# A 96-byte constant tile at the top of the right side of SBUF in a kernel of Fourier mixing and a gated feed-forward layer

## The chip, the cores and the metric

The kernel runs on one core of one Trainium2 chip. The metric is the device time of one execution in microseconds (us). Three executions of the kernel before the change took 755.44, 754.17 and 755.10 us; the median is 755.1 us.

## The reference

For an input x of 2048 rows and 512 columns, everything in fp32:

```python
a = x @ dft_hid_re.T                      # (2048, 512)
b = x @ dft_hid_im.T
y = dft_seq_re @ a - dft_seq_im @ b       # DFT matrices of 2048 x 2048
out_b = (silu(x @ w1) * (x @ w3)) @ w2    # w1, w3: 512 x 1376, w2: 1376 x 512
g = sigmoid((x * gate_w).sum(-1))
return g * y + (1 - g) * out_b
```

## The kernel before

**Arithmetic.** Every fp32 operand of a matrix product is split into two parts, a rounded high part (type fp32r) and the rest. `split` (L109) does it: ScalarE copies the source into the high part (L110), VectorE subtracts that from the source for the low part (L111). `mm3` (L113) then issues three matmuls, high by high, high by low and low by high, all at L115. Each has a stationary operand of 128x128 and a moving operand of 128x512, both fp32r in SBUF, and adds into a bank of PSUM. So nearly the whole of TensorE's work is one kind of instruction at one line: a weight load and a matmul of 512 columns, 3,078 times. [...] The products are grouped in a Strassen-like scheme of seven half-size products with sums of operands in front, which VectorE forms.

**Stages.** (1) Gate and up (about 0 to 236 us): the stationary operands are weights (tiles `wa` and `wb`, made from w1 and w3), the moving operand is x transposed, in the large tiles `xo0` for the first 1024 rows and `xo1` for the other 1024. The list ITEMS (L156) sets the order: first nine chunks with `xo0`, then chunks 9 and 10 with both halves in turn, then nine with `xo1`. The first item is done by `plain` (L336) with other small tiles, `b12` and `a21`. Each of the other 21 items is seven products with 42 matmuls in all, into the tiles X, Y and Z. (2) From about 236 us on, 182 steps (`step`, L687) of up to twelve matmuls each, into tiles named P: blocks 0 to 3 multiply with the sequence DFT (the moving operand is `zo`, split from blocks B of the input cc; the stationary operand is `a`, the tiles `a1` and `a2`), blocks 4 and 5 (H) are the product with w2, blocks 6 and 7 (Y) the hidden DFT and the output. A block of the kind F goes through seven products (P1, P5, P6, P3, P7, P2, P4) of four steps each; H has three and Y two steps for each product.

**What sets the order around the matmuls.** TensorE and the DMA queue of SyncE follow the order in which the code issues. In the second part everything does (L567). `advance` (L553), called in each step, loads blocks ahead, forms the sums (`sum_c`, L518) and splits the operand of the step three ahead (`split_c`, L530). There are four `zo` tiles. After the split of a block B22, the queue of GpSimd issues a DMA that adds another block onto it in place (L543); the result is split for the product P7, which comes one product later.

**Where the tiles lie.** SBUF is filled from both ends of each partition: pools opened with side "left" grow from the low end, pools with side "right" from the high end. In the kernel as built, the left side begins at byte 1152, which is 9 x 128. The first tile on the right is the constant `act0` (L118), 128 x 1 fp32, which lies at byte 229,312, which is 64 more than a multiple of 128. Every tile behind it on either side is a multiple of 2048 bytes. So every operand tile on the left starts at a multiple of 128, and every one on the right 64 bytes past one; slices of operands start at multiples of 512 bytes within a tile. On the left lie `xo0`, `b12`, `a21`, two of the four `zo` tiles (`zo_0`, `zo_1`), and seven of the eight tiles `a1` (later those of H and Y in their places). On the right lie `wa`, `wb`, `xo1`, the `zo` tiles `zo_2` and `zo_3`, the eighth `a1`, and all tiles `a2`. A matmul takes its two operands from the same side or from two sides, as these places give it:

- gate and up with `xo0`: moving left, stationary right;
- gate and up with `xo1`: both right;
- second part: all four combinations, in runs of 12 or 24 matmuls.

`act0` itself holds nothing that is used: one Silu (L334) writes it at the start from the zeros of the tile `warm`, and nothing reads it.

Of the kernel before, what the change touches and what calls it, by code (L numbers as in the profile page):

```python
# [7 lines left out]
F32 = mybir.dt.float32  # L8
F32R = mybir.dt.float32r
AF = mybir.ActivationFunctionType  # L10
ALU = mybir.AluOpType

P = 128
# [20 lines left out]
def fnet_swiglu_gate_kernel(  # L34
# [20 lines left out]
    nc = tc.nc  # L55
# [12 lines left out]
    const = ctx.enter_context(tc.tile_pool(name="const", bufs=1, side="right"))  # L68
# [46 lines left out]
            nc.tensor.matmul(ps, u, v, start=first and n == 0, stop=last and n == 2,  # L115
                             skip_group_check=chain)

    act0 = const.tile([P, 1], F32, tag="act0", name="act0")  # L118
    nbsp = dram.tile([D, S], F32, tag="nbsp", name="nbsp")
    gs = dram.tile([NTB, 1, 512], F32, tag="gs", name="gs")  # L120
    gsp, ngsp = (dram.tile([2, P, 1024], F32, tag=k, name=k) for k in ("gsp", "ngsp"))
# [207 lines left out]
    warm = s1p.tile([P, 1024], mybir.dt.bfloat16, tag="s1", name="warm")[:, :512]  # L329
    nc.vector.memset(warm, 0.0)  # L330
    wps = bank(7, "wps")
    for n in range(WARM):
        nc.tensor.matmul(wps, warm[:, :P], warm, start=True, stop=True)
    nc.scalar.activation(act0, warm[:, :1], AF.Silu)  # L334

    def plain(b12, a21):  # L336

# [511 lines left out]
```

## Time and profile before

| what | value |
|---|---|
| median of three executions | 755.1 us (754.17 to 755.44) |
| the profiled execution | 754.2 us; its span 752.4 us |
| granted TensorE clock, mean | 0.993 |
| TensorE matmul busy | 97% of the span, 3,089 matmuls |
| VectorE busy | 76% |
| ScalarE busy | 49% |
| DMA | 186.17 MB, mean 247 GB/s |

The span is the time from the first to the last instruction of the profiled execution; 1.8 us of its time lie outside. A matmul's row has a start and a duration, but matmuls overlap in the pipeline: one of 512 columns is shown with about 390 ns, while the next one starts about 230 ns after it. What a matmul costs the kernel is the distance from start to start, so rows of a timeline that merge six equal matmuls are read by their starts, six distances apart. An idle time at an engine is put down to the instruction whose semaphore came last.

### The profile page before, as it was taken

Reading aid. Unit: us, or ns where it says so; the run is one execution under the profiler, and the core shown is the slowest. Engines: PE = TensorE matmul, PEld = TensorE weight load, DVE = VectorE, ACT = ScalarE, POOL = GpSimd, SP = SyncE. Lnnn points to the kernel's source line nnn. Section 1 sums busy time; section 2 is a strip of 40 time slices with the busy share of each in tenths; the row PEclk is TensorE's granted clock in tenths of the full one; section 3 lists DMA queues with packets and bytes.
Section 4 is the critical chain, followed back from the end, with each engine's and each line's share of the span. In section 5 each row is a group of like instructions: output and inputs, shape, how many; then the busy total and the mean of one; then the engine's idle time right before and its main releaser. Section 6 shows DMA issues by size and latency. Waiting matters only on the chain.

```text
span 752.4 us, 8533 instructions
## 1 busy us (share of the span) xinstructions
PE 726.2 (97%) x3089; PEld 580.0 (77%) x3089; DVE 574.7 (76%) x715; ACT 367.0 (49%) x485; POOL 52.4 (7%) x76
## 2 busy tenths in 40 slices
PE   9999999989897899999999999999999999999996
PEld 5777888878675677888788878887878878887775
DVE  6989895467574997887698769884976695885956
ACT  6665564445433665345453545444435454453423
POOL 0111111101010010001000010001001001000000
PEclk9999999999999999999999999999999999999999
DMA  6575682368869757775957495829999599696862
GB/s 251 172 303 218 249 331 101 108 216 310 326 225 420 263 148 230 267 284 160 267 215 274 134 284 211 309 88 272 360 417 372 153 337 294 219 346 199 310 162 90
DMA packets 49626, 186.17 MB, mean 247 GB/s; under 512 B 5168, under 2 KB 5296, under 8 KB 44976
## 3 DMA queue, kind: packets, MB, share of 16 engines
q1 hardware_dynamic: 39440, 142.10, 52.0%
q0 software_dynamic: 9856, 43.00, 19.3%
q8 instruction: 24, 0.39, 0.2%
q10 hardware_dynamic: 288, 0.52, 0.2%
q14 instruction: 18, 0.15, 0.1%
HBM read 128.45 MB, written 57.16 MB: 247 GB/s over the span
## 4 chain that ended last, share of the span: by engine, by line
PE 31%; issue 24%; DMA 21%; DVE 16%; ACT 6%; SPq 1%; POOL 1%; POOLq 0%; ACTq 0%; DVEq 0%
PE P L115 19%; DMA B<-cc 8%; PE X L115 7%; DVE zo L111 5%; ACT zo L110 4%; DMA B<-zsp 3%; DMA xr<-xn 3%; PE Z L115 3%; DVE B L527 2%; PE Y L115 2%; DMA B<-hsp 1%; DMA dsp<-late 1%; PE C L115 1%; DMA nb<-nbsp 1%; DMA gs<-sc 1%
## 5 line engine op out<-in xcount | busy, mean ns | idle before, releaser
L115 PE MATMUL P<-zo,a 128*128 128x512 f32 x1344 | 314.7, 394 | 8.5 <-DVE zo L111 5.1
L115 PEld LDWEIGHTS P<-zo,a 128*128 128x128 f32 x1344 | 252.2, 188 | 71.1 <-DVE zo L111 10.5
L110 ACT ACTIVATE zo<-B 128x1024 fp32r<-128x1024 f32 (+1 forms) x182 | 187.7, 1043 | 218.1 <-PE P L115 76.7
L111 DVE TENSOR_TENSOR zo<-B,zo 128x1024 fp32r<-128x1024 f32 (+1 forms) x182 | 216.9, 1203 | 98.1 <-ACT zo L110 97.4
L115 PE MATMUL P<-zo,H 128*128 128x512 f32 x468 | 107.9, 392 | 0.2 <-DVE zo L111 0.2
L115 PEld LDWEIGHTS P<-zo,H 128*128 128x128 f32 x468 | 87.7, 188 | 20.2 <-DVE zo L111 0.6
L115 PE MATMUL X<-xo,wb 128*128 128x512 f32 x378 | 95.4, 396 | 4.2 <-DVE u L290 3.2
L527 DVE TENSOR_TENSOR B<-B,B 128x1024 f32<-128x1024 f32 (+1 forms) x78 | 92.8, 1190 | 2.5 <-DMA B<-hsp 2.4
L115 PEld LDWEIGHTS X<-xo,wb 128*128 128x128 f32 x378 | 71.4, 190 | 22.1 <-DVE u L290 4.5
L115 PE MATMUL P<-zo,Y 128*128 128x512 f32 x336 | 80.5, 400 | 3.2 <-ACT zu L726 2.7
L115 PEld LDWEIGHTS P<-zo,Y 128*128 128x128 f32 x336 | 63.8, 191 | 19.8 <-ACT zu L726 3.1
L115 PE MATMUL X<-xo,wa 128*128 128x512 f32 x126 | 33.9, 401 | 3.5 <-ACT h L297 2.7
L115 PE MATMUL Z<-xo,wa 128*128 128x512 f32 x126 | 32.7, 395 | 0.8 <-ACT u L287 0.8
L115 PE MATMUL Y<-xo,wa 128*128 128x512 f32 x126 | 32.6, 393 | 0.0
L115 PE MATMUL Z<-xo,wb 128*128 128x512 f32 x126 | 32.5, 392 | 0.0
L115 PEld LDWEIGHTS X<-xo,wa 128*128 128x128 f32 x126 | 23.7, 190 | 9.8 <-ACT h L297 3.3
L290 DVE TENSOR_TENSOR u<-u,X 128x512 f32<-128x512 f32 x21 | 14.4, 684 | 20.3 <-PE X L115 20.0
L115 PEld LDWEIGHTS Z<-xo,wa 128*128 128x128 f32 x126 | 23.4, 188 | 7.1 <-ACT u L287 1.9
L115 PEld LDWEIGHTS Y<-xo,wa 128*128 128x128 f32 x126 | 23.7, 188 | 5.4
L115 PEld LDWEIGHTS Z<-xo,wb 128*128 128x128 f32 x126 | 23.6, 188 | 5.3
L543 POOL DMA_DIRECT2D B<-cc x16 | 13.7, 858 | 200.5 <-DVE zo L111 186.6
L110 ACT ACTIVATE wa<-ws 128x768 fp32r<-128x768 f32 (+2 forms) x21 | 17.0, 810 | 19.0 <-PE Z L115 11.8
(106 smaller groups left out, 529.5 us busy)
## 6 DMA issues: line engine op xcount, KB each, us to landing
B<-cc SPq DMA_DIRECT2D x64, 512.0 KB, 6.8
hsp<-h POOLq DMA_DIRECT2D x22, 512.0 KB, 5.9
B<-hsp SPq DMA_DIRECT2D x20, 512.0 KB, 9.6
wbsp<-wb POOLq DMA_DIRECT2D x8, 1024.0 KB, 5.7
wb<-wbsp SPq DMA_DIRECT2D x8, 1024.0 KB, 5.2
B<-cc POOLq DMA_DIRECT2D x16, 512.0 KB, 10.4
B<-zsp SPq DMA_DIRECT2D x16, 512.0 KB, 7.7
H<-w2sp SPq DMA_DIRECT2D x6, 1024.0 KB, 10.2
```

The costliest lines, as they stand in the source:

```text
L110: nc.scalar.activation(hi, src, AF.Copy)
L111: nc.vector.tensor_sub(lo, src, hi.bitcast(F32))
L115: nc.tensor.matmul(ps, u, v, start=first and n == 0, stop=last and n == 2, skip_group_check=chain)
L290: nc.vector.tensor_add(u4, u4, x)
L527: nc.vector.tensor_add(t, t, RAW[blk, b, q][:, :n])
L543: nc.gpsimd.dma_start(src, block(blk, "B12", q), accum_op=ALU.add)
```

## The change

The constant tile `act0` takes 24 columns in place of one, 96 bytes in place of 4 in each partition, and the Silu that fills it takes 24 columns of `warm`. The tile of 4 bytes begins at byte 229,312; that of 96 bytes takes 64 bytes more of the allocation and begins at 229,248, which is 1791 x 128. All other tiles of the right side lie 64 bytes lower than before, and so at multiples of 128. The left side is as it was, and the two sides do not meet: the least distance between them is 832 bytes before the change. Nothing else is touched.

```diff
-    act0 = const.tile([P, 1], F32, tag="act0", name="act0")
+
+    act0 = const.tile([P, 24], F32, tag="act0", name="act0")
...
-    nc.scalar.activation(act0, warm[:, :1], AF.Silu)
+    nc.scalar.activation(act0, warm[:, :24], AF.Silu)
```

## The prediction

> **What bounds the kernel now.** I read the engine table first, then the timeline of TensorE in stretches with no stop in them, then the chain that ended last, and last the table by stretches. The page's first line of busy times:
>
> ```profile
> PE 726.2 (97%) x3089; PEld 580.0 (77%) x3089; DVE 574.7 (76%) x715; ACT 367.0 (49%) x485; POOL 52.4 (7%) x76
> ```
>
> TensorE is taken for 97% of the 752.4 us, and it does one thing: a matmul of 512 columns, 3,078 times. Where it isn't stopped, the time of the kernel is the distance from one matmul's start to the next's, times their number. So the question is whether that distance hangs on where the operands lie. The timeline of TensorE in the first product shows it with one moving tile and two stationary ones:
>
> ```profile
> 9.94 2.60 PE L115 MATMUL C<-xo,wa 128*128 128x512 f32 x10 [0.29 <-DVE xo L111]
> 12.38 1.56 PE L115 MATMUL C<-b,wa 128*128 128x512 f32 x6
> 13.78 1.53 PE L115 MATMUL C<-b,a 128*128 128x512 f32 x6
> 15.15 0.63 PE L115 MATMUL C<-xo,wa 128*128 128x512 f32 x2
> ```
>
> Six matmuls of `b12` (left) with `wa` (right) take from 12.38 to 13.78, 1.40 us, 233 ns for each. Six with the same moving tile and `a21` (left as well) take from 13.78 to 15.15, 1.37 us, 228 ns. Longer stretches of the gate and up stage are sharper. First with `xo0` on the left and the weights on the right, then with `xo1` and the weights both on the right:
>
> ```profile
> 60.33 1.56 PE L115 MATMUL Z<-xo,wb 128*128 128x512 f32 x6
> ...
> 74.32 1.56 PE L115 MATMUL Z<-xo,wa 128*128 128x512 f32 x6
> ```
>
> ```profile
> 169.50 1.52 PE L115 MATMUL Z<-xo,wb 128*128 128x512 f32 x6
> ...
> 180.38 1.52 PE L115 MATMUL X<-xo,wa 128*128 128x512 f32 x6
> ```
>
> In the first, 60 matmuls (the rows between are 6, 6, 6, 6, 12, 6, 6 and 6) start within 13.99 us: **233.2 ns**. In the second, 48 (6, 6, 6, 6, 12, 6 and the first 6) start within 10.88 us: **226.7 ns**. Instruction, shapes, types and engine order are equal; what differs is that the operands lie 64 bytes off each other modulo 128 in the first and agree in the second. In `b12` with `a21` both are at 0, in `xo1` with the weights both at 64: that they agree is what the fast pairs have in common, not that they are at 0.
>
> The second part mixes the four combinations. Its longest piece without a stop, from the chain of work that ended last:
>
> ```profile
> 604.06 66.25 PE P L115 x287
> ```
>
> From the first start to the last end 66.25 us; less the 0.16 us by which a last matmul is shown longer than its distance (390 less 230 ns), 66.09 / 287 = **230.3 ns**, between the two values above, as a mixture must be.
>
> **The change part by part.** *The Silu on act0.* It takes 24 columns in place of one. ScalarE's rows at the start:
>
> ```profile
> 2.03 0.20 ACT L334 ACTIVATE act<-warm 128x1 f32<-128x1 bf16 x1
> 3.16 0.42 ACT L110 ACTIVATE wa<-ws 128x256 fp32r<-128x256 f32 x1 [0.93 <-DMA ws<-w]
> ```
>
> One column takes 0.20 us, 256 take 0.42, so 24 take some 0.02 more, in the 0.93 us in which ScalarE waits for its first weights anyway. If that cover went, it would cost 0.02 us. Nothing reads the tile. I count nothing.
>
> *The other engines.* They read and write the moved tiles too. ScalarE's groups by shape, with results on the left (`b`) and on the right (`wb`):
>
> ```profile
> L110 ACT ACTIVATE b<-xs_B 128x1024 fp32r<-128x1024 f32 x1 | 1.1, 1061 | 0.2 <-DMA xs_B<-xt 0.2
> L110 ACT ACTIVATE wb<-wu 128x1024 fp32r<-128x1024 f32 x11 | 11.6, 1057 | 2.3 <-DVE wu L220 2.3
> ```
>
> 1061 ns at 0 and 1057 at 64 modulo 128: no difference to speak of. For VectorE and the DMA queues no row separates the places so cleanly; no instruction is added or moved there, and I count nothing for them, with up to 1 us on either side left to the range.
>
> *The matmuls.* All operands of both sides now agree modulo 128. I take 226.7 ns for every matmul that isn't stopped, the value of pairs that agree, and work out what this takes off TensorE.
> - Gate and up with `xo0`: ten of the 21 items of 42 matmuls, and 36 of the 48 of the first item. 456 x (233.2 - 226.7) = 3.0 us. The items with `xo1` agree already and gain nothing.
> - The second part: 1344 + 468 + 336 = 2,148 matmuls of tiles P. 2,148 x (230.3 - 226.7) = 7.7 us.
>
> That is 10.7 us less work on TensorE, and the upper end. What doesn't reach the end is worked out by stage, from the table by stretches (per row: PE, PEld, DVE, ACT, POOL busy, granted clock, share of DMA, GB/s):
>
> ```profile
> 25.00:60.00 35.00, 32.62 (x138) 25.34 (x137) 31.56 (x45) 22.55 (x31) 3.08 (x5) 1.00 0.65 247
> 202.00:230.00 28.00, 26.22 (x105) 20.76 (x106) 17.34 (x31) 11.21 (x21) 4.17 (x6) 0.94 0.72 254
> 230.00:260.00 30.00, 24.34 (x93) 17.89 (x92) 22.08 (x30) 15.73 (x21) 1.84 (x3) 0.94 0.94 368
> 260.00:300.00 40.00, 39.40 (x169) 31.27 (x168) 32.67 (x43) 23.16 (x33) 3.45 (x4) 1.00 0.63 178
> 500.00:550.00 50.00, 49.24 (x215) 39.82 (x213) 35.10 (x40) 23.84 (x30) 3.42 (x4) 1.00 0.87 283
> 735.00:752.40 17.40, 13.07 (x48) 10.00 (x48) 12.59 (x13) 4.85 (x6) 0.00 (x0) 0.90 0.24 91
> ```
>
> - *25 to 60 us*: VectorE is busy for 31.56 of 35 us, and TensorE stops for 2.4 us. 137 matmuls x 6.5 ns = 0.9 us are to be had; where VectorE is the link, a faster TensorE only stops longer. Of 0.9 I let half go: 0.45 us lost.
> - *230 to 300 us*: the stage changes over; TensorE stands for 5.7 and 0.6 us, and the chain runs through the splits on ScalarE and VectorE and the loads (DMA at 0.94). 262 matmuls x 3.6 ns = 0.9 us, of which I let 0.7 go.
> - *The blocks after it*: TensorE is busy for 49.24 of the 50 us from 500 on, with short stops, and one pattern returns in them. From the chain, in the second block:
>
> ```profile
> 351.73 10.25 DMA B<-cc
> 361.99 0.02 issue
> 362.01 1.07 ACT zo L110
> ...
> 367.78 1.24 DVE zo L111
> 369.01 0.04 issue
> 369.06 3.06 PE P L115 x12
> ```
>
> GpSimd's adding DMA (L543) is issued at 351.73, when the block B22 has been split, takes 10.25 us, and its result must be split before the product P7 can start. Between the two lie one product's four steps of TensorE, 48 matmuls, 11.1 us at 230.3 ns. The DMA and the splits don't get shorter; TensorE's part does, by 48 x 3.6 = 0.17 us, and the stop at P7 grows by as much. One such link in each of the eight blocks: 8 x 0.17 = 1.4 us lost. SyncE's loads are issued further ahead (`advance` loads eight steps ahead); one that comes late costs in the same way and is in the range.
>
> Sum: 10.7 - 0.45 - 0.7 - 1.4 = 8.1 us. From the profiled execution's own 754.2 us that gives 746.1; that execution lies 0.9 us under the median of the three, so the forecast as a median is 755.1 - 8.1 = **747.0 us**, 1.1% faster.
>
> [...]
>
> **The rivals.** *The places don't matter* (what differs between the stretches is something else, such as which tiles VectorE and the DMAs touch meanwhile, or which half of SBUF is read): nothing changes, 755.1 us. For it speaks that pairs from two sides are the slow ones, so that the side itself could be the cause and not the 64 bytes. Against the first reason: the rows of six start 1.40 and 1.36 us apart all through the two stretches, in which the other engines start and stop. Against the second I have only that 64 bytes are a plainer difference than a side. 10 in 100.
>
> *The gain is eaten by loads and splits.* For it: DMA is busy for 0.87 of the stretch 500 to 550 us and 0.94 at the change of stages, and every block's chain goes through DMA waits such as the 10.25 us above. If the whole second part ran at the pace of the DMAs, only the gate and up stage's 3.0 - 0.45 = 2.5 us would stay: 752.6 us. Against it: TensorE stands for less than 2% of that part, so it is still what sets the pace between the stops. With half of the second part's remaining 5.6 us kept, 755.1 - 2.5 - 2.8 = 749.8. 13 in 100, at 749.5 to 753.
>
> *Slower: pairs across the sides meet worse.* All pairs seen to run at 226.7 ns come from one side, where the distance between operands is a multiple of 512 bytes. Across the sides it is now 192 or 320 modulo 512, and after the change it will be 256, which no row shows. If the reads collide by a larger period than 128 bytes, these pairs could fall on a slower step. They are 456 in gate and up and some 1,050 in the second part (counted from the tiles' places). One step of 6.5 ns more than today costs 1,500 x 6.5 = 9.8 us, half a step 4.9; on TensorE's path nothing hides it. Taken in between, nearer to the half: 761 us. It decides from the point where a pair across the sides takes longer than it does today (233.2 ns in gate and up). For it speaks only that the period is unknown; against it, that two places 64 bytes apart already make the whole difference. 7 in 100.
>
> *The clock* changes each of these by a step: in the stretches of 28, 30 and 17.4 us with 0.94, 0.94 and 0.90 the granted clock was down for 28 x 0.06 = 1.7 us of full speed each. If stops shift, one such window may go or come: 1.7 us on either side.
>
> **How the numbers follow.** Forecast 70 in 100, with a range of its own of 747.0 less and plus 2.7 (one clock window, 1 us for loads): 744.3 to 749.7. Gain eaten 13, places don't matter 10, slower 7. The range for 8 in 10 is the forecast's and the eaten gain's, 744.0 to 752.6. A measurement of this kernel can tell about 0.2%, 1.5 us, from no change: faster than that has 70 and 13, 0.83; the same 0.09; slower, with a little of the unchanged cases, 0.08.
>
> **What would show it.** In gate and up with `xo0`, rows of six matmuls should start 1.36 us apart in place of 1.40; those with `xo1` stay at 1.36. A long piece of P in the chain should come to 227 ns for each matmul in place of 230.3. If gate and up quickens and P doesn't, P's pairs are the ones to ask. The starts of P7 should wait longer than now, by about 0.2 us. If the distances fall and the time doesn't, the stops have grown and the gain was eaten; if the distance with `xo0` stays at 233.2, it is the side that counts; above it, the third rival.

## The result and the profile after

The changed kernel takes 749.56 us (median of four executions, 748.86 to 750.54) against 754.85 us before; the ratio is 0.9931 with a 95% interval of 0.9914 to 0.9948, so it is faster by 5.2 us (3.9 to 6.5). The forecast was 747.0 us, 8.1 us faster. Its range holds the result; its size is off by a third, and, as the experiments show, its rule for which places are fast was wrong.

Line numbers from L118 on are one higher than before. TensorE's timeline in gate and up with `xo0`, where six matmuls took 1.40 us:

```profile
59.40 1.52 PE L115 MATMUL Z<-xo,wb 128*128 128x512 f32 x6
60.76 1.52 PE L115 MATMUL X<-xo,wa 128*128 128x512 f32 x6
62.12 1.52 PE L115 MATMUL X<-xo,wb 128*128 128x512 f32 x6
63.48 1.52 PE L115 MATMUL Z<-xo,wa 128*128 128x512 f32 x6
64.84 1.52 PE L115 MATMUL Y<-xo,wa 128*128 128x512 f32 x6
```

24 starts in 5.44 us are 226.7 ns for each, in place of 233.2. The longest pieces of the second part, from the chain that ended last:

```profile
368.50 76.28 PE P L115 x335
...
601.78 70.80 PE P L115 x311
```

(76.28 - 0.16) / 335 is 227.2 ns, the other gives 227.1, where the piece of before gave 230.3. So TensorE's distances did what the prediction said of them, in both stages. The Silu on act0 costs 0.02 us in ScalarE's wait at the start, as expected:

```profile
2.03 0.22 ACT L335 ACTIVATE act<-warm 128x24 f32<-128x24 bf16 x1
3.14 0.42 ACT L110 ACTIVATE wa<-ws 128x256 fp32r<-128x256 f32 x1 [0.89 <-DMA ws<-w]
```

**Where the rest went.** From the starts of the 3,078 matmuls at L115 each trace can be split into three: what distances up to 245 ns hold over 226.7 ns; what longer ones hold in stretches whose granted clock is 0.50 (427 ns for a matmul); and the stops. (The page's other eleven matmuls, at L333, take 1.19 to 5.66 us before the change, most of them 427 ns apart.) In us:

```
trace                      longer distances   half clock   stops   span
before                          10.4              3.8       30.6   752.4
after                            1.3              7.4       32.3   748.8
after, second trace (e1)         1.0              3.3       33.9   745.8
```

The border between the last two columns is good to about 0.8 us, since a matmul can lie partly in a half-speed stretch or behind a stop. The distances give back 9.1 and 9.4 us. The stops take 1.7 and 3.3 of it. The half-speed clock takes 3.6 us more in one trace of the changed kernel and 0.5 less in the other. The table by stretches shows where: before (its row from 230 us on stands in the prediction), after, and the second trace (the numbers behind the busy times are granted clock, share of DMA and GB/s).

```profile
150.00:205.00 55.00, 50.28 (x216) 40.39 (x215) 37.75 (x67) 26.02 (x45) 4.90 (x7) 0.98 0.80 287
```

```profile
150.00:205.00 55.00, 49.75 (x205) 39.57 (x204) 37.59 (x66) 25.22 (x43) 4.90 (x7) 0.95 0.78 274
...
230.00:260.00 30.00, 25.07 (x93) 19.14 (x93) 21.51 (x29) 15.76 (x22) 1.84 (x3) 0.89 0.94 369
```

```profile
150.00:205.00 55.00, 49.98 (x215) 39.52 (x214) 39.41 (x69) 26.38 (x46) 4.89 (x7) 1.00 0.78 282
...
230.00:260.00 30.00, 25.18 (x93) 19.02 (x92) 24.37 (x33) 17.03 (x23) 1.84 (x3) 0.89 0.83 323
```

In 150 to 205 us the clock stood at 0.98, 0.95 and 1.00. The first trace of the changed kernel loses 55 x 0.05 = 2.8 us of full speed there, where the kernel before loses 55 x 0.02 = 1.1, and starts the second part at 237.0 us, later than before the change (236.5); the second trace loses nothing there and starts it at 233.5.

### The profile page after: what moved, and what is told of

Read it like the earlier page. It is cut to its first block, busy times and chain, and to the rows that moved or that the text cites. A ratio compares the mean times of both kernels' runs of the same rounds, so it can differ in the third digit from the quotient of the medians.

```text
span 748.8 us, 8533 instructions
## 1 busy us (share of the span) xinstructions
PE 721.0 (96%) x3089; PEld 581.9 (78%) x3089; DVE 574.4 (77%) x715; ACT 366.4 (49%) x485; POOL 52.4 (7%) x76
## 4 chain that ended last, share of the span: by engine, by line
PE 40%; issue 20%; DMA 19%; DVE 14%; ACT 5%; POOL 1%; SPq 1%; POOLq 0%; ACTq 0%; DVEq 0%
PE P L115 27%; PE X L115 7%; DMA B<-cc 5%; DVE zo L111 5%; DMA B<-hsp 3%; DMA B<-zsp 3%; ACT zo L110 3%; PE Z L115 3%; PE Y L115 2%; DVE B L528 2%; DMA H<-w2sp 2%; DMA xr<-xn 2%; PE C L115 1%; DMA xs_B<-xt 1%; DMA gs<-sc 1%
## 5 line engine op out<-in xcount | busy, mean ns | idle before, releaser
L115 PE MATMUL P<-zo,a 128*128 128x512 f32 x1344 | 311.7, 393 | 7.8 <-DVE zo L111 4.7
L115 PEld LDWEIGHTS P<-zo,a 128*128 128x128 f32 x1344 | 253.5, 189 | 66.0 <-DVE zo L111 8.9
L115 PE MATMUL P<-zo,H 128*128 128x512 f32 x468 | 107.3, 390 | 0.9 <-DVE zo L111 0.8
L115 PEld LDWEIGHTS P<-zo,H 128*128 128x128 f32 x468 | 87.5, 188 | 20.5 <-DVE zo L111 2.5
L115 PE MATMUL X<-xo,wb 128*128 128x512 f32 x378 | 96.1, 399 | 5.1 <-DVE u L291 3.8
L115 PEld LDWEIGHTS X<-xo,wb 128*128 128x128 f32 x378 | 72.1, 192 | 23.0 <-DVE u L291 5.4
L115 PE MATMUL P<-zo,Y 128*128 128x512 f32 x336 | 79.5, 397 | 3.7 <-ACT zu L727 3.0
L115 PEld LDWEIGHTS P<-zo,Y 128*128 128x128 f32 x336 | 63.8, 191 | 19.2 <-ACT zu L727 3.5
L115 PE MATMUL X<-xo,wa 128*128 128x512 f32 x126 | 33.7, 400 | 4.2 <-ACT h L298 3.4
L115 PE MATMUL Z<-xo,wa 128*128 128x512 f32 x126 | 32.3, 391 | 0.5 <-ACT u L288 0.4
L115 PE MATMUL Z<-xo,wb 128*128 128x512 f32 x126 | 32.2, 389 | 0.0
L115 PE MATMUL Y<-xo,wa 128*128 128x512 f32 x126 | 32.2, 389 | 0.0
L115 PEld LDWEIGHTS X<-xo,wa 128*128 128x128 f32 x126 | 23.8, 191 | 10.4 <-ACT h L298 4.2
L115 PEld LDWEIGHTS Z<-xo,wa 128*128 128x128 f32 x126 | 23.4, 188 | 6.3 <-ACT u L288 1.4
L115 PEld LDWEIGHTS Z<-xo,wb 128*128 128x128 f32 x126 | 23.8, 189 | 5.1
L115 PEld LDWEIGHTS Y<-xo,wa 128*128 128x128 f32 x126 | 23.6, 188 | 4.9
## 6 DMA issues: line engine op xcount, KB each, us to landing
B<-hsp SPq DMA_DIRECT2D x20, 512.0 KB, 10.3
```

## The experiments

The question that came first: is the fast place one where the operands agree modulo 128, and which stage gives the gain?

**e1: the changed kernel again.**

> The changed kernel once more, for a narrower interval and a second trace. All theories: about 749.5 us, 0.993 of before. If the half-speed clock windows (five of 3.4 us in the first trace, three before the change) hang on chance, this trace has another number of them, and each one fewer goes with 1.7 us less.

Measured: 749.77 us, ratio 0.9931 (0.9905 to 0.9958), and the second trace above: three half-speed stretches of 3.4 us in place of five, and 747.59 us against 750.54. Over all ten executions of the two jobs the mean granted clock is 0.9907; in 23 executions of the kernel before, on the chip of e1 to e4, it is 0.9926. 0.0019 x 752 us is 1.4 us of clock, lost on average on that chip. On the three chips of the later runs the kernel before itself has 0.9910, 0.9919 and 0.9909, so that this doesn't show that the change lowers the clock.

**e2: both sides at 64 modulo 128.**

```diff
+    padl = ctx.enter_context(tc.tile_pool(name="padl", bufs=1, side="left"))
+    padl.tile([P, 16], F32, tag="padl", name="padl")
```

> Everything as before the change, but 64 unused bytes lie at the low end of the left side, so that the operands of both sides lie 64 bytes past a multiple of 128. Theory (the operands of one matmul must agree modulo 128): 226.7 ns from start to start everywhere and the same time as the changed kernel, about 749.5 us. Rival (each operand must lie at a multiple of 128): every matmul is as slow as or slower than now, 755 us or more. Rival (pairs from two sides are slow): no change, 754.9 us.

Measured: 748.67 us, ratio 0.9924 (0.9900 to 0.9948). Its timeline in gate and up and its longest piece of the second part:

```profile
60.64 1.52 PE L117 MATMUL X<-xo,wa 128*128 128x512 f32 x6
62.00 1.52 PE L117 MATMUL X<-xo,wb 128*128 128x512 f32 x6
63.36 1.52 PE L117 MATMUL Z<-xo,wa 128*128 128x512 f32 x6
```

```profile
598.66 70.84 PE P L117 x311
```

1.36 us for six, and 227.3 ns in the second part. No operand of these products lies at a multiple of 128, and the gain is there. So multiples of 128 as such, the reason in the change's own words, are not what makes it fast. Nor do pairs from two sides cost anything as such: 227.4 and 226.9 ns on average in this trace.

**e3 and e4: one stage alone.** e3 holds 64 unused bytes on the right through gate and up, e4 from there on:

```diff
+    pad_cm, pad = pool("pad", 1, "right")
+    pad.tile([P, 16], F32, tag="pad", name="pad")
     ws_cm, wsp = pool("ws", LOOK + 1, "right")
...
-    gate_pools = (ws_cm, wu_cm, s1_cm, wa_cm, wb_cm, u4_cm, h_cm, xo1_cm)
+    gate_pools = (pad_cm, ws_cm, wu_cm, s1_cm, wa_cm, wb_cm, u4_cm, h_cm, xo1_cm)
```

> 64 unused bytes on the right side for the time of the gate and up stage alone, so that its pairs agree and those of the second part don't. Theory (the end of the gate and up stage is set by its loads and splits): TensorE has 3.0 us less to do there, but the second part starts no earlier, and the time is 754 to 755 us. Rival (the gate and up stage kept its gain and the second part lost some): 752 to 753 us.

> The same 64 bytes from the second part on alone. Theory (the gate and up stage gives nothing to the end): as fast as the changed kernel or faster by the clock window that its gate and up stage gained, 748 to 749.5 us. Rival (both stages give their share): 751 to 752 us.

Measured: e3 753.25 us, ratio 0.9984 (0.9965 to 1.0004); e4 751.93 us, ratio 0.9964 (0.9945 to 0.9983). My theory, formed on the first trace of the changed kernel, fell: e4's interval, 750.5 to 753.4 us, leaves out the 748 to 749.5 us of it. So the second part alone is not the whole gain. e3's interval reaches no change, and its time lies between the two ranges expected, so that the times alone don't show the share of gate and up. The traces do for TensorE: what distances up to 245 ns hold over 226.7 ns, 10.4 us before the change, is 7.5 in e3 and 3.9 in e4. The two medians add up to 1.2 + 2.7 = 3.9 us, which agrees with 5.2 within the intervals. The first trace had misled me, since it has a half-speed stretch at 155 us, which the kernel before hasn't, besides one at 203 us, which both have.

**e5, e6, e7 and e10: other distances.** act0 with 16, 32, 56 and 40 columns puts the right side at 32, 96, 0 and 64 modulo 128, each time in the same two lines as the change:

```diff
-    act0 = const.tile([P, 1], F32, tag="act0", name="act0")
+    act0 = const.tile([P, 56], F32, tag="act0", name="act0")
...
-    nc.scalar.activation(act0, warm[:, :1], AF.Silu)
+    nc.scalar.activation(act0, warm[:, :56], AF.Silu)
```

> act0 with 16 columns (64 bytes): the operands of the right side lie 32 bytes past a multiple of 128, those of the left at multiples. Theory (both must agree modulo 128): the pairs from two sides stay slow, in gate and up with the left half of x above 226.7 ns, and the time is 752 to 757 us. Rival (agreeing modulo 32 is enough): 226.7 ns everywhere and the time of the changed kernel, 749.5 us.

> act0 with 32 columns (128 bytes): the right side lies 96 bytes past a multiple of 128. Theory as for 32 bytes: pairs from two sides slow, 752 to 757 us; by the sign of the distance the two kinds of pair (moving left with stationary right, and the reverse) may change places. Rival (agreeing modulo 32 is enough): 749.5 us.

> act0 with 56 columns (224 bytes): the right side lies at multiples of 128 again, 128 bytes lower than in the changed kernel, so that the distance between operands of two sides is another one modulo 256 and 512. Theory (only the place modulo 128 counts): 226.7 ns for all pairs and the time of the changed kernel, 749.5 us. Rival (a larger period, by which the changed kernel's distance was a lucky one): pairs from two sides above 228 ns, 752 us or more.

> act0 with 40 columns (160 bytes): the right side lies 64 bytes past a multiple of 128 as before the change, but 128 bytes lower, so that the distance of right to left is 192 modulo 256 where it was 64. Theory (the distance modulo 256 counts, with its sign): pairs from two sides stay slow, and the two kinds change places: moving left with stationary right about 230 ns, moving right with stationary left 233.3; 754 to 756 us, for gate and up with the left half of x quickens by 1.4 us and the second part slows by as much. Rival (only the place modulo 128 counts): 233.3 and 230.3 ns as before the change.

Measured: e5 755.16 us, ratio 1.0003 (0.9987 to 1.0019); e6 755.80, 1.0008 (0.9989 to 1.0028); e7 754.94, 1.0009 (0.9992 to 1.0027); e10 752.81, 0.9984 (0.9967 to 1.0001). e7 is the decisive one. All its operands lie at multiples of 128 on both sides, just as in the change, only 128 bytes lower on the right. Its timeline in gate and up, and the piece of the second part that corresponds to the prediction's:

```profile
60.65 1.56 PE L115 MATMUL Z<-xo,wb 128*128 128x512 f32 x6
...
74.62 1.56 PE L115 MATMUL Z<-xo,wa 128*128 128x512 f32 x6
```

```profile
605.99 66.42 PE P L115 x287
```

60 matmuls (6, 6, 6, 6, 6, 12, 6, 6 and 6) in 13.97 us are 232.8 ns, and the second part has 66.26 / 287 = 230.9: as slow as before the change. The period is not 128. In e10 the six matmuls come 1.37 or 1.38 us apart, neither the slow 1.40 nor the fast 1.36:

```profile
69.52 1.54 PE L115 MATMUL Z<-xo,wb 128*128 128x512 f32 x6
70.90 1.54 PE L115 MATMUL X<-xo,wa 128*128 128x512 f32 x6
72.27 1.54 PE L115 MATMUL X<-xo,wb 128*128 128x512 f32 x6
```

The means of the distances (those up to 245 ns) for pairs from two sides, about 930 with the moving operand on the left and about 520 with it on the right in each trace, set against the place of the stationary operand less that of the moving one, modulo 256:

```
stationary less moving   moving left, stationary right   moving right, stationary left
  0                      227.4 (after), 227.4 (e2)       226.9 (after), 226.9 (e2)
 32                      233.2 (e5)                      233.2 (e6)
 64                      233.3 (before)                  233.3 (e10)
128                      232.8 (e7)                      232.3 (e7)
192                      229.6 (e10)                     230.3 (before)
224                      233.3 (e6)                      233.4 (e5)
```

The two columns agree to 0.7 ns. In these traces the side doesn't matter, nor does the place of one operand; the distance does, with its sign (233.3 ns at 64, 229.6 and 230.3 at 192), modulo 256. Before the change it was 64 and 192, the change makes it 0. A multiple of 256 is enough here: the change's own distance is 256 modulo 512, and its 24 starts above give the 226.7 ns of the prediction's pairs of one side, which lie at a multiple of 512. That the slow rows repeat every 256 bytes too is shown for 128 alone (128 and 384 modulo 512); each of the others was run at one distance modulo 512. In these long runs the next matmul's stationary operand, whose load overlaps the running matmul (PE and PEld are busy for 97% and 77% of the span before the change), lies as far from the moving operand as the matmul's own, so the table doesn't tell which of the two counts.

e10's time misses the 754 to 756 us expected. Gate and up quickened as expected, but the second part didn't slow by as much: it has 516 and 528 matmuls of the two kinds of pair (counted from the tiles' places), so that their change of places costs it nearly nothing. e10's trace has 8.8 us of longer distances against 10.4 before the change.

**e8, e9 and e11: the stops of the second part.** The prediction let the adding DMA ahead of P7 eat part of the gain. e8 puts P2 ahead of P7, so that two products cover that DMA (10.25 us in the prediction's rows):

```diff
-             ("P7", "T3"), ("P2", "B21"), ("P4", "T4"))
+             ("P2", "B21"), ("P7", "T3"), ("P4", "T4"))
...
-    ORDER = [CHAIN] * (NB - 1) + [tuple(CHAIN[i] for i in (0, 5, 1, 2, 3, 4, 6))]
+    ORDER = [CHAIN] * NB
```

with B21 loaded one product earlier (and the last block in the same order as the others). e9 is the same order without the change's places.

> The changed kernel with the product P2 ahead of P7 in every block, so that two products, not one, lie between the split of B22 and that of its sum, which the adding DMA of about 10 us forms. Theory (the stops of the second part come from that DMA, and ate about 1.5 us of the gain): the stops at P7 go, those of the blocks 1 to 4 (together 4 us) and most of the one at 731 us with its clock window, and the time falls to 741 to 746 us. Rival (another late load takes the place): 748 to 751 us.

> The kernel before with the product order of e8 alone; act0 and all places as before the change. Theory (the stops at P7 hide part of the gain of the places): without them the places are worth nearly all of the 9 us that TensorE saves, so this takes 750.5 to 752 us against 742.7 with the places of the change. Rival (the places are worth the same 5 us with either order): 747 to 748.5 us.

Measured: e8 742.66 us, ratio 0.9846 (0.9817 to 0.9874); e9 748.38, 0.9927 (0.9901 to 0.9954). The stops at P7 are gone: a piece without a stop goes from 542 us to the end of TensorE's work.

```profile
542.11 195.05 PE P L115 x852
```

What TensorE waited for in P, in total, times and longest, in the changed kernel and in e8:

```profile
PE P L115 <- DVE zo L111: 6.0, 12, 0.8
...
PE P L115 <- ACT zu L727: 3.0, 1, 3.0
PE P L115 <- ACT zo L110: 2.9, 1, 2.9
```

```profile
PE P L115 <- ACT zu L726: 5.0, 3, 2.0
...
PE P L115 <- ACT zo L110: 2.9, 1, 2.9
PE P L115 <- DVE zo L111: 2.0, 3, 0.8
```

The twelve waits for the splits shrink to three, and the one of 3.0 us in the last block goes too. In their place stand three new ones in the blocks 1 to 3, 5.0 us in all: P4 must not add to its bank before ScalarE has read P7 from it, and P2 used to lie between. ScalarE reads late there because its queue holds another split, which waits for a DMA of 5.25 us:

```profile
378.80 5.25 DMA w2sp<-late
384.06 0.02 issue
384.08 0.02 ACTq L110
384.10 0.04 issue
384.14 1.06 ACT zo L110
385.20 0.49 ACT zu L726
385.69 0.04 issue
385.74 4.38 PE P L115 x18
```

The two orders together say how much of the gain the stops at P7 had hidden: with the new order the places are worth 748.38 - 742.66 = 5.7 us (6.1 by the two ratios, each taken on its own chip), with the old one 5.2. So the times don't show that the stops had hidden any of it, and e9's median lies outside the 750.5 to 752 us of my theory. They don't rule out a part either: from the two intervals, the 6.1 us can be 3 to 9. The traces tell more. In the blocks H and Y (4 to 7), what distances above 245 ns hold over 226.7 ns, stops and half clock together, is 6.5 us before the change, 8.4 in both traces of the changed kernel, and nothing in e9 and e8. So with the old order the stops there did take 1.9 us more after the change. The new order gives that back, but e8 loses as much elsewhere: the traces of e9 and e8 have 10.3 and 0.7 us of longer distances, 2.6 and 5.4 of half clock, 24.9 and 26.9 of stops. Of the 9.7 us saved, the clock takes 2.9 and the stops, in gate and up and in the blocks F, 2.0. The mean granted clock, 0.9935 in six executions of e9 and 0.9908 in five of e8, differs by some 2.0 us, but the two ran on different chips.

e11 leaves the blocks F in their order and changes H and Y alone.

> The changed kernel with P2 ahead of P7 in the blocks H and Y alone; the blocks F keep their order. In e8 TensorE stood three times for 1.5 to 2.1 us at P4 in the blocks F, where P7's result must be read from its bank before P4 may add to it, and no longer at P7. Theory (the new order only trades one stop for another in the blocks F, and gains in H and Y): as e8 or up to 2 us faster, 740.5 to 743 us. Rival (the blocks F gained too): 743.5 to 746 us.

Measured: 740.80 us, ratio 0.9806 (0.9777 to 0.9835). It is the fastest of all, as the theory has it; its interval meets that of e8, so that the 2 us between them are not certain. The traces agree with the theory for the blocks F: what distances above 245 ns hold there (blocks 1 to 3) is 4.1 and 4.7 us in the changed kernel, 4.8 in e11 and 7.4 in e8. The mean granted clock of e11, 0.9947 on another chip, is 0.0039 above that of e8, or 2.9 us, the whole difference and more.

## Why the prediction was right and where it was not

- **What bounds the kernel** was right. TensorE's start-to-start distance is the time where nothing stops it, and it hangs on the operands' places: 226.7 to 233.4 ns.
- **"That they agree is what the fast pairs have in common"** was right, but the step that made it a rule, agreement modulo 128, was wrong. The rows had only three distances: multiples of 512, and 64 and 192 modulo 256. They could not tell 128 from 256. The changed kernel's distance of 768 bytes is a multiple of 256 by the size of what lies in between; with act0 larger by 128 bytes (e7, ratio 1.0009) the same title would fit the change and it would bring nothing. That the forecast went the right way was luck in this step. A longer period is what the third rival supposed, to which I gave 7 in 100 with "two places 64 bytes apart already make the whole difference" against it: that argument was no argument, since a longer period shows the same at 64 bytes.
- **10.7 us off TensorE**: 9.1 and 9.4 in the two traces. The gate and up stage gave 2.8 of its 3.0. For the second part I took the mean of one piece, 3.6 ns for each matmul; over all 2,148 the excess was 7.1 us in place of 7.7. And 1.0 to 1.3 us of longer distances stay, mostly in the first matmuls after a stop (1.2 of the 1.3 us in the first ten).
- **2.55 us lost to stops**: 1.7 and 3.3. The size was about right, its reasons in part. The eight links at P7 were the term of 1.4 us. By their own rule they are 1.1, since a product has 36 matmuls in H and 24 in Y, not 48. Measured, the stops grew by 1.9 us in the blocks H and Y (half clock in them included), in P7 and in the products after it, and hardly in the blocks F (3.8 us before, 4.1 and 4.7 after, in the blocks 1 to 3). In gate and up they grew by about 1.5 us, most of it past 60 us, where I had put nothing. Nor were the stops of the second part "less than 2%" of it: they are about 15 us in 516, 3%.
- **The clock**, which I left out of the sum and put into the range with 1.7 us on either side. 9.2 us off TensorE less 2.5 to stops is 6.7, just over the interval of 3.9 to 6.5 around the 5.2 us measured. With the 1.4 us of clock lost on the chip of e1 to e4 it is 5.3. So the clock is the term that closes the sum, but it is not shown that the change lowers it: traces with the places of the change have five, three, four, four and two half-speed stretches of 3.4 us (after, e1, e2, e8, e11), those with slow places three, five, three, three, two and two (before, e5, e6, e7, e10, e9).

The half-speed stretches (granted clock 0.50) between the first 6 us and TensorE's last matmul all last 3.4 us or twice that, and the same kernel had five of them in one trace and three in another. In all thirteen traces each begins within 5 us after the start of a stop of 1.9 us or longer. The stops of about 3.0 us at the change of stages are followed by one in all of them; others only sometimes: the stop of 2.9 us near 200 us is followed by one in the first trace of the changed kernel and not in the second. So in these traces the number of stretches goes with a few long stops: e8, e9 and e11, without the stop of about 3 us in the last block, have none in that block.

Why the distance between TensorE's two operands counts is open: no run shows it. Shown is only what hangs on it, 226.7 to 233.4 ns for a matmul.

## What to carry to other kernels

Where a matmul with its own weight load is the bound, read start-to-start distances by operand pair, and try other distances between the stationary and the moving operand. Here a multiple of 256 bytes gave 226.7 ns against up to 233.4 at others, for 512 columns of fp32r, and 64 unused bytes on one side were enough for it. A saving that a trace shows in full on the bounding engine need not reach the end in full: of 9 us, longer stops and, as far as the traces tell, stretches at half clock took four, and one trace alone can put the loss into the wrong stage. Before trusting a rule read from a few places, ask which other rule the same places would fit, and try the place that tells the two apart.

## What the runs showed of the hardware

- The time of a matmul stream went with the operands' distance and its sign (stationary less moving, modulo 256): over the 226.7 ns of a distance of 0 (changed kernel, e2), 192 cost about 3 ns for each matmul (229.6 in e10, 230.3 before), 32, 64, 128 and 224 about 6 (232.3 to 233.4 in e5, e6, e7, e10 and before).
- In the trace of before the stream took some ten matmuls to settle after a change of pairing: in the second part pairs of one side took 230 to 232 ns on average in the first four, and 227 from the eleventh on. In gate and up, where the pairing stays, the rows of six are 1.36 or 1.40 us apart for ten microseconds and more (169.50 to 180.38 and 60.33 to 74.32 us).
- In the thirteen traces half-speed stretches of the clock (granted 0.50), 3.4 us or twice that, came only behind a stop of TensorE of 1.9 us or longer; stops of 2.98 us and more always had one behind them, and the longest without one is 2.92 us (e9).
- The place of its result made no difference to ScalarE's copy of 128x1024 into the high part (tiles `b` and `wb`): 1061 ns at 0 and 1057 at 64 modulo 128 before the change, 1063 and 1057 with both at 0 after it.
